# One block-diagonal product for two heads: a change in the attention stage of a fused attention and expert kernel

## The chip, the cores and the metric

The kernel runs on one core of one Trainium2 chip. Its time is the device time in microseconds of one execution. The time before is the median of three timed runs, 858.31 us. A profiled execution, recorded by the hardware profiler, gives the trace from which all rows below are taken.

The core has a matrix engine (PE; its weight loads, which overlap the products, are listed as PEld), a vector engine (DVE), a scalar engine (ACT), a general engine (POOL), a queue engine that issues most transfers (SP), and 16 DMA engines. Each engine runs its instructions in program order and waits where an operand isn't there yet.

## The reference

Three layers follow each other, all in 32-bit floats.

- Attention on q, k, v of 4 batches, 8 heads, 576 positions, 64 columns. It is the sum of two attentions. One works on means over groups of 4 positions (144 of them), and its output is repeated 4 times. The other is local: each position looks at the positions less than 4 away.
- A mixture of 8 experts on the 2,304 tokens of 512 columns: logits of the normalised token, the best expert, its softmax weight, two matrix products with a relu between them.
- A dense layer: 512 to 2,048, leaky relu, 2,048 to 512.

```python
out_d = sm_attn(q_d, k_d, v_d)             # on means of 4 positions
out_up = np.repeat(out_d, factor, axis=2)
mask = np.abs(pos[:, None] - pos[None, :]) < factor
...
out_local = np.matmul(attn, v)
return (out_up + out_local).astype(np.float32)
```

## The kernel before

The program has two stages. Up to about 189 us it does attention and the choice of experts (the routing), then the experts and the dense layer, where PE works without pause.

**Order.** The attention stage runs in an order written out by hand: the string `ORDER`, a list of items such as `LV.6`, each a call of a small function (`todo` has the table). On PE, DVE, ACT and POOL the instructions stand in exactly this order. Transfers on SP also follow the order in which they are called, and SP waits at each until its buffer is free. Items behind `at(...)` calls later in the program are sorted by planned times; they belong to the second stage.

**Local attention.** The 2,304 tokens are 18 tiles of 128. A tile has 4 strips of 32 positions; each strip looks at a window of 38 positions. Heads are handled as 4 pairs (`n`), head `n` and head `n + 4`; the member of the pair is `s`. `S.t` computes the scores, `SMX`, `SSB`, `SEX`, `SSM`, `SNM` the softmax, `LT.t` transposes it (PE) and `LTE.t` evicts it as `leT` (ACT): the 64 rows of member 0 stand on partitions 0 to 63, those of member 1 on 64 to 127. `LV.t` (`lo_pv`) adds two things in one PSUM tile `psLV`:

- the reduced attention's output for these tokens, repeated 4 times by a product with a 0/1 matrix (`rep_w`, or `rem_w` for the last 16 groups of a batch), in two parts (`dn_h` and `dn_l`, which together carry the value in the format of the fast products). These are called the carry products here;
- the local product: for each pair, member and strip a product of 64 rows by 32 array columns with v's window, 64 columns moving. Each 32-bit product is recorded as two, so these are 64 products of a tile.

`LX.t` (`lo_x`) copies the result to the tile `xt`, `LAD.t` stores it, `X`, `XE`, `L`, `LG`, and for each three tiles `LD` (picks the expert), `PF` (ranks, on PE), `PD`, `SC` route the tokens.

**v's windows.** `vw.g` (`load_vw`) loads the windows of 9 strips, half a batch, into one of three buffers `vws`, 10 or 12 transfers on SP. Group g serves strips 9g to 9g + 8: LV.2 reads groups 0 and 1, LV.4 groups 1 and 2, LV.6 groups 2 and 3, LV.15 groups 6 and 7. The buffers are cleared once by DVE at the start.

**Reduced attention.** `ds.b.u` (`dn_score`) computes scores of a batch's half, `dm`, `db`, `dx` the softmax, `dT`, `dE` transpose it, `dv.b.u` (`dn_pv`, L439 and L445) multiplies with v's means, `do`, `dh`, `dl` scale and split the output.

**Spare products.** `keep` makes products with zeros whose result nobody reads. `NW` of them (22) run before the first data arrive; an item with `+n` runs n more ahead of its own products. 8 stand before `T.0.0.0.0`, 15 before `LV.17`, 7 before `PF.17`; the 4 named at `XT.0` are never issued, since that function has no such call.

**First expert's weights.** `WL.u` loads quarter u (0 to 3) of the first expert's weights into one of two raw buffers, `WH.u.i.c` (ACT) and `WO.u.i.c` (DVE) split it into two fast parts in a buffer of 16 KB per partition (`w_unit`). Quarters 0 and 1 lie in a pool `wa` with two buffers, opened at `early`; quarters 2 and 3 in `wb`, opened at `cut`, when the attention's memory is given back. `XT`, `XH`, `XO` prepare the first tokens, `L1`, `RL`, `RO`, `L2` compute.

Of the kernel before, what the change touches and what calls it, by code (L numbers as in the profile page):

```python
# [21 lines left out]
NP = H // 2  # L22
# [31 lines left out]
O = dict(QM=(0, 0, 1, 1), NQ=8, NQD=2, NDE=0, NC=0, NVD=2, NVW=3, NES=3, NW=22, TO=12, TS=11, HB=2, XF=4, XL=3.0, WL=4,  # L54
# [3 lines left out]
qk.0.0.0 ce cv qk.0.1.0 vg.0.1 qk.0.0.1 qk.1.1.1 emb cm qk.0.1.1 cr vg.0.0 T.0.0.0.0+8 qk.1.0.1 T.0.0.0.2 E.0.0.0.0  # L58
# [14 lines left out]
E.2.1.1.1 L.3 db.1.1 S.7 SNM.6 LTE.4 LG.3 P.2.1.1 dv.1.0 dx.1.1 ds.2.0 v.2.0 SMX.7 dT.1.1.0 do.1.0 T.2.0.1.1 dE.1.1.0
SSB.7 dT.1.1.1 E.2.0.1.1 dT.1.1.2 dh.1.0 SEX.7 S.8 dm.2.0 dE.1.1.2 dl.1.0 X.1 dE.1.1.1 P.2.0.1 db.2.0 T.3.1.0.0 XE.1
dv.1.1 SMX.8 dx.2.0 E.3.1.0.0 SSB.8 v.2.1 T.3.1.1.0 SSM.7 SEX.8 dT.2.0.0 LAD.1 T.3.1.0.2 do.1.1 LAD.0 dE.2.0.0 ds.2.1
vg.3.0 E.3.1.0.2 E.3.1.1.0 qk.3.0.1 dh.1.1 SSM.8 dT.2.0.1 LAD.2 T.3.1.1.1 dE.2.0.1 dl.1.1 T.3.0.0.0 LAD.3 SNM.8 L.1
vg.3.1 E.3.1.1.1 dm.2.1 T.3.0.0.1 SNM.7 E.3.0.0.0 LV.5 LG.1 E.3.0.0.1 db.2.1 dv.2.0 LX.5 LD.2 v.3.0 dx.2.1 LV.4 LAD.5
# [5 lines left out]
SSM.10 SQ.7 LT.9 XE.7 SP.8 PF.5 dm.3.0 T.3.0.1.2 LTE.9 S.12 PD.5 SNM.10 E.3.0.1.2 L.7 db.3.0 SC.5 LT.10 LG.7 T.3.0.1.1
SMX.12 dx.3.0 LV.9 LAD.7 RN.8 early LTE.10 SSB.12 E.3.0.1.1 SEX.12 dT.3.0.0 LD.8 LX.9 LT.11 dE.3.0.0 LV.10 LAD.9
SSM.12 P.3.0.1 SQ.9 LTE.11 LM.8 S.14 LE.8 LX.10 SE.8 PF.8 SNM.12 X.9 LAD.10 SQ.10 SMX.14 ds.3.1 PD.8 XM XE.9 SSB.14
dT.3.0.1 SC.8 dm.3.1 LT.12 SEX.14 LV.11 dE.3.0.1 SSM.14 LTE.12 db.3.1 X.10 vw.6 LX.11 dv.3.0 XE.10 SNM.14 X.11 SQ.11
do.3.0 L.9 dx.3.1 SP.11 S.13 XE.11 RN.11 dT.3.1.0 LG.9 SMX.13 dh.3.0 L.11 dE.3.1.0 SSB.13 dT.3.1.1 LAD.11 dl.3.0 LG.11
# [10 lines left out]
WO.3.1.0 L2.3 WO.3.0.1 RL.5 RO.5 WO.3.0.0 L1.4 XB L1.7 RL.4 RO.4 L2.4 L1.6 L2.5 GB BT.0 RL.7 RL.6 BT.1 RO.7 BH.0 RO.6
BT.2 BH.1 BO.0 L2.6 BO.1 BH.2 BO.2 BT.3 L2.7 BH.3 BO.3
# [10 lines left out]
def tile_kernel(ctx, tc, q, k, v, emb, tau, w1, w2, win, wout, out):  # L110
# [51 lines left out]
    with man:  # L162
# [28 lines left out]
        vws = [ac.tile([P, NP, GS, D], F32, name="vw%d" % i) for i in range(O['NVW'])]  # L191
# [119 lines left out]
        def load_vw(g):  # L311
# [3 lines left out]
            for s in range(2):  # L315
                part = t[64 * s:64 * s + 64]
# [67 lines left out]
        def dn_score(b, u):  # L384
            ps = psA.tile([P, 2, 512], F32, name="psD", tag="A")
            idle(ps[:, 0, 0:256], dn_score, b, u)
            for r in range(2):
                for c in range(0, P, 64):
                    for s in range(2):
                        T.matmul(ps[c:c + 64, s, r * GR:(r + 1) * GR], qd[b][64 * s:64 * s + 64, 2 * u + r, c:c + 64],  # L390
                                 kd[b][64 * s:64 * s + 64, 2 * u + r, :], start=True, stop=True)
            if u:
                for n in range(NP):
                    for s in range(2):
                        T.matmul(ps[32 * n:32 * n + 32, s, 2 * GR:3 * GR],
                                 qd[b][64 * s:64 * s + 64, n, GR - 32:], kd[b][64 * s:64 * s + 64, n, :],
                                 start=True, stop=True)
            sps[b, u] = ps
# [31 lines left out]
        def dn_pv(b, u):  # L430
# [109 lines left out]
        def lo_pv(t):  # L540
# [9 lines left out]
            for s in range(2):  # L550
                for z, (b, r, p0) in enumerate(segs):
                    for w, src in enumerate((dn_h[b], dn_l[b])):
                        if r < 4 * P:
                            T.matmul(ps[:, s, 0:256], rep_w[:, HW + r - p0:HW + r - p0 + P],
                                     src[:, 0:DM].rearrange("p (i a d) -> p a i d", i=2, a=2)[:, s],
                                     start=z == 0 and w == 0, stop=False, skip_group_check=True)
                        else:
                            for n in range(NP):
                                T.matmul(ps[:, s, n * D:(n + 1) * D], rem_w[:, n, HW - p0:HW - p0 + P],
                                         src[:, DM + s * D:DM + (s + 1) * D],  # L560
# [753 lines left out]
```

## Time and profile before

| | |
|---|---|
| timed runs | 859.88, 858.31, 855.56 us; median 858.31 |
| profiled execution | 853.95 us |
| its span, first to last instruction | 852.2 us |
| mean granted clock of PE | 0.971 |
| PE, busy share and products | 95%, 7,887 |
| DVE, ACT, POOL, busy share | 54%, 40%, 25% |
| bytes moved | 97.88 MB |

A busy share is a mean over both stages. PE's products are pipelined, and a busy PE isn't a PE at its peak. Two products that follow each other are compared by their starts. A row of the timeline merges neighbouring instructions of one kind: start, length of the whole group, engine, line, what is written from what, rows and columns, number, and in brackets the idle time before the group with what ended it. "Issue" there means that nothing which the profile shows was awaited.

### The profile page before, as it was taken

The numbers are of one execution on the slowest core, as the hardware profiler recorded it, in microseconds if no ns is written. First come the engines' busy times: TensorE is split into PE (matmuls) and PEld (weight loads), VectorE is DVE, ScalarE is ACT, GpSimd is POOL, SyncE is SP. The second block draws the span as 40 slices with busy tenths as digits, with TensorE's granted clock in tenths as the row PEclk, the third lists the DMA queues.
The fourth block names the chain that finished last, engine by engine and source line by source line (L and its number), as shares of the span: only waits on it lengthen the run. The fifth ranks groups of instructions, "written<-read, shape, count | busy, mean of one in ns | idle before, by whom it ended". The sixth has DMA issues, their size and how long they took to land. (4 is left out here: it accounts for less than half of the span.)

```text
span 852.2 us, 19006 instructions
## 1 busy us (share of the span) xinstructions
PE 810.4 (95%) x7887; PEld 742.1 (87%) x7887; DVE 462.5 (54%) x902; ACT 337.2 (40%) x686; POOL 210.7 (25%) x244
## 2 busy tenths in 40 slices
PE   7878999789999999999999999999999999999995
PEld 6767787679999999999997789999999999999994
DVE  6646655544377988897579992332332232232222
ACT  3445645544454555656433232322223222222221
POOL 8465534234033234323023420101001001001001
PEclk9989978979999999999999999999999999999998
DMA  9779654545476787797634410111011011000001
GB/s 266 172 173 193 157 124 98 140 131 123 102 267 191 258 237 212 237 293 238 211 113 125 136 50 1 37 38 38 1 38 38 0 38 38 1 1 38 0 1 40
DMA packets 104652, 97.88 MB, mean 115 GB/s; under 512 B 58956, under 2 KB 83148, under 8 KB 104562
## 3 DMA queue, kind: packets, MB, share of 16 engines
q1 hardware_dynamic: 94018, 69.88, 29.8%
q0 software_dynamic: 10544, 26.74, 9.9%
q8 instruction: 64, 1.05, 0.5%
q14 instruction: 26, 0.21, 0.1%
HBM read 81.48 MB, written 15.12 MB: 113 GB/s over the span
## 5 line engine op out<-in xcount | busy, mean ns | idle before, releaser
L923 PE MATMUL psh<-xhi,w 128*128 128x384 f32 (+9 forms) x672 | 215.9, 321 | 0.0
L924 PE MATMUL psh<-xlo,w 128*128 128x384 f32 (+9 forms) x672 | 215.6, 321 | 0.0
L925 PE MATMUL psh<-xhi,w 128*128 128x384 f32 (+9 forms) x672 | 215.2, 320 | 0.0
L955 DVE SCALAR_TENSOR_TENSOR hs<-hs 128x384 f32<-128x384 f32 x96 | 61.9, 645 | 185.8 <-ACT hs L954 185.8
L923 PEld LDWEIGHTS psh<-xhi,w 128*128 128x128 f32 x672 | 127.7, 190 | 4.0
L924 PEld LDWEIGHTS psh<-xlo,w 128*128 128x128 f32 x672 | 127.7, 190 | 3.9
L925 PEld LDWEIGHTS psh<-xhi,w 128*128 128x128 f32 x672 | 127.6, 190 | 0.0
L954 ACT COPY hs<-psh 128x384 f32<-128x384 f32 x96 | 45.9, 478 | 194.5 <-PE psh L925 191.6
L1008 PE MATMUL pso<-w,hh 128*128 128x512 f32 x282 | 112.9, 400 | 3.7 <-ACT hh L960 3.1
L1009 PE MATMUL pso<-w,hh 128*128 128x512 f32 x282 | 110.9, 393 | 0.0
L1039 POOL DMA_INDIRECT out_dram<-o,tk x18 | 18.0, 999 | 320.9 <-ACT o L1038 315.4
L869 DVE TENSOR_TENSOR w<-r,w 128x1024 fp32r<-128x1024 f32 (+1 forms) x72 | 83.1, 1159 | 11.0 <-ACT w L866 10.6
L960 ACT CAST hh<-hs 128x384 fp32r<-128x384 f32 x94 | 48.2, 513 | 93.2 <-DVE hs L955 93.2
L996 PE MATMUL psy<-hh,w 128*128 128x192 f32 (+8 forms) x288 | 81.9, 306 | 0.0
L1006 PE MATMUL pso<-w,hl 128*128 128x512 f32 x282 | 80.8, 393 | 0.0
L997 PE MATMUL psy<-hh,w 128*128 128x192 f32 (+8 forms) x288 | 79.4, 298 | 0.0
L911 POOL TENSOR_TENSOR ds<-r 128x512 f32<-128x512 f32 x32 | 42.5, 1327 | 145.8 <-DVE r L909 63.5
L961 DVE TENSOR_TENSOR hl<-hs,hh 128x384 fp32r<-128x384 f32 x94 | 52.4, 557 | 45.8 <-ACT hh L960 45.8
L975 ACT ACTIVATE hh<-psh 128x192 fp32r<-128x192 f32 (+8 forms) x72 | 29.2, 405 | 110.4 <-PE psh L925 107.3
L866 ACT CAST w<-r 128x1024 fp32r<-128x1024 f32 (+1 forms) x72 | 67.6, 947 | 3.5 <-DMA r<-in_moe_w_dram 3.5
L1008 PEld LDWEIGHTS pso<-w,hh 128*128 128x128 f32 x282 | 52.9, 188 | 16.9 <-ACT hh L960 7.9
L1006 PEld LDWEIGHTS pso<-w,hl 128*128 128x128 f32 x282 | 53.0, 188 | 12.9 <-DVE hl L961 0.3
(230 smaller groups left out, 1255.2 us busy)
## 6 DMA issues: line engine op xcount, KB each, us to landing
r<-in_moe_w_dram SPq DMA_DIRECT2D x64, 512.0 KB
r<-in_moe_w_in_dram POOLq DMA_DIRECT2D x16, 512.0 KB, 5.3
r<-in_moe_w_out_dram POOLq DMA_DIRECT2D x16, 512.0 KB, 5.0
vw<-in_v_dram SPq DMA_DIRECT2D x64, 96.0 KB
vg<-in_v_dram SPq DMA_DIRECT2D x8, 576.0 KB
x_d<-xt SPq DMA_DIRECT2D x18, 256.0 KB
yc<-yT_d SPq DMA_DIRECT2D x6, 768.0 KB
qk<-in_q_dram SPq DMA_DIRECT2D x4, 576.0 KB
```

The source lines that it names most:

```text
L866: A.copy(w[:, 0, i, cs], src)
L869: V.tensor_tensor(out=w[:, 1, i, cs], in0=src, in1=w[:, 0, i, cs].bitcast(F32), op=ALU.subtract)
L923: T.matmul(ps, lh, rh, start=start, stop=False)
L924: T.matmul(ps, lh, rl, start=False, stop=False)
L925: T.matmul(ps, ll, rh, start=False, stop=stop)
L955: V.scalar_tensor_tensor(out=hs, in0=hs, scalar=0.01, in1=hs, op0=ALU.mult, op1=ALU.max)
L961: V.tensor_tensor(out=gl[:, 0:n], in0=hs, in1=gh[:, 0:n].bitcast(F32), op=ALU.subtract)
L996: T.matmul(ps, wh, hh[:, 0:n], start=f == 0, stop=False, skip_group_check=True)
L997: T.matmul(ps, wl, hh[:, 0:n], start=False, stop=False, skip_group_check=True)
L1006: T.matmul(ps, hl[:, c], wh, start=False, stop=f == NF2 - 1, skip_group_check=True)
L1008: T.matmul(ps, hh[:, c], wh, start=f == 0, stop=False, skip_group_check=True)
L1009: T.matmul(ps, hh[:, c], wl, start=False, stop=False, skip_group_check=True)
```

## The change

- In `lo_pv` the two heads of a pair are one product. v's window becomes a tile with the two members on a block diagonal (member s on partitions 64 s to 64 s + 63 and in columns 64 s to 64 s + 63, zeros elsewhere), the weights are all 128 rows of `leT`, and 128 columns move. The carry products take both members at once as well, so one PSUM bank holds the tile's output in the order pair, member, column. `dn_pv` writes its heads in that order, and `lo_x` puts them back.
- `dn_score` uses weights of 128 columns in place of two times 64.
- The buffers of v's windows are twice as large, and there are two of them instead of three. In the order, group 1 is loaded where group 2 was, and groups 2, 3, 5 and 7 are each loaded just behind the last product that reads the buffer: `LV.2 vw.2`, `LV.4 vw.3`, `LV.7 vw.5`, `LV.13 vw.7`. Group 4 stays behind LV.6 and group 6 goes just behind LV.11.
- To make room, `wa` has one buffer until `cut`, and quarter 1 of the first expert's weights goes to a new pool `wc` opened there. Its conversions `WH.1.*` and `WO.1.*`, which stood among the items of tiles 15 to 17, now stand together behind `XH.3` and ahead of `LD.17`.
- The counts `+8`, `+15`, `+4` and `+7` are gone. The 22 spare products ahead of the first load stay.

The order string is cut here to the items that matter; nothing else in it moves but these.

```diff
-O = dict(QM=(0, 0, 1, 1), NQ=8, NQD=2, NDE=0, NC=0, NVD=2, NVW=3, NES=3, NW=22, TO=12, TS=11, HB=2, XF=4, XL=3.0, WL=4,
+O = dict(QM=(0, 0, 1, 1), NQ=8, NQD=2, NDE=0, NC=0, NVD=2, NVW=2, NES=3, NW=22, TO=12, TS=11, HB=2, XF=4, XL=3.0, WL=4,
...
-qk.0.0.0 ce cv qk.0.1.0 vg.0.1 qk.0.0.1 qk.1.1.1 emb cm qk.0.1.1 cr vg.0.0 T.0.0.0.0+8 qk.1.0.1 T.0.0.0.2 E.0.0.0.0
+qk.0.0.0 ce cv qk.0.1.0 vg.0.1 qk.0.0.1 qk.1.1.1 emb cm qk.0.1.1 cr vg.0.0 T.0.0.0.0 qk.1.0.1 T.0.0.0.2 E.0.0.0.0
...
-WH.1.0.0 LAD.16 X.16 SQ.16 WO.1.0.0 XE.16 XR WH.1.0.1 LTE.17 WO.1.0.1 LG.14 LV.17+15 WH.1.1.1 LD.14 WH.1.1.0 WO.1.1.1
...
+XO.2 LG.17 XH.3 WH.1.0.0 WO.1.0.0 WH.1.0.1 WO.1.0.1 WH.1.1.1 WH.1.1.0 WO.1.1.1 WO.1.1.0 LD.17 XO.3 PF.17 LM.17 L1.0
...
-        vws = [ac.tile([P, NP, GS, D], F32, name="vw%d" % i) for i in range(O['NVW'])]
+        vws = [ac.tile([P, NP, GS, 2, D], F32, name="vw%d" % i) for i in range(O['NVW'])]
...
-                part = t[64 * s:64 * s + 64]
+                part = t[64 * s:64 * s + 64, :, :, s]
...
-                for c in range(0, P, 64):
-                    for s in range(2):
-                        T.matmul(ps[c:c + 64, s, r * GR:(r + 1) * GR], qd[b][64 * s:64 * s + 64, 2 * u + r, c:c + 64],
-                                 kd[b][64 * s:64 * s + 64, 2 * u + r, :], start=True, stop=True)
+                for s in range(2):
+                    T.matmul(ps[:, s, r * GR:(r + 1) * GR], qd[b][64 * s:64 * s + 64, 2 * u + r, 0:P],
+                             kd[b][64 * s:64 * s + 64, 2 * u + r, :], start=True, stop=True)
...
-                        T.matmul(o[c:c + 64, n, :], eT[:, n, kc, c:c + 64], vd[b][:, kc, head(2 * u + n % 2, n // 2), :],
+                        T.matmul(o[c:c + 64, 2 * (n % 2) + n // 2, :], eT[:, n, kc, c:c + 64], vd[b][:, kc, head(2 * u + n % 2, n // 2), :],
...
+            for z, (b, r, p0) in enumerate(segs):
+                for w, src in enumerate((dn_h[b], dn_l[b])):
+                    first = z == 0 and w == 0
+                    if r < 4 * P:
+                        T.matmul(ps[:, 0], rep_w[:, HW + r - p0:HW + r - p0 + P], src[:, 0:DM],
+                                 start=first, stop=False, skip_group_check=True)
+                    else:
+                        for n in range(NP):
+                            T.matmul(ps[:, 0, 2 * n * D:2 * (n + 1) * D], rem_w[:, n, HW - p0:HW - p0 + P],
+                                     src[:, DM:DM + 2 * D], start=first and n == 0, stop=False, skip_group_check=True)
...
-                for s in range(2):
-                    for c, b, sg, w0 in strips(t):
-                        w = vwt[b * (NSTRIP // GS) + sg // GS][:, :, sg % GS]
-                        T.matmul(ps[32 * c:32 * c + 32, s, n * D:(n + 1) * D],
-                                 eT[64 * s:64 * s + 64, n, 32 * c:32 * c + 32], w[64 * s:64 * s + 64, n, :],
-                                 start=False, stop=True, skip_group_check=True)
+                for c, b, sg, w0 in strips(t):
+                    w = vwt[b * (NSTRIP // GS) + sg // GS]
+                    T.matmul(ps[32 * c:32 * c + 32, 0, 2 * n * D:2 * (n + 1) * D], eT[:, n, 32 * c:32 * c + 32],
+                             w[:, n, sg % GS].rearrange("p s d -> p (s d)"), start=False, stop=True, skip_group_check=True)
...
-            on("LX").copy(x.rearrange("p (s c) -> p s c", s=2), st_.pop(('V', t))[:, :, 0:256])
+            on("LX").copy(x.rearrange("p (s n d) -> p n s d", s=2, d=D),
+                          st_.pop(('V', t))[:, 0].rearrange("p (n s d) -> p n s d", s=2, d=D))
...
-            for nm, bufs in (("wa", 2), ("xa", 1), ("rp", 1)):
+            for nm, bufs in (("wa", 1), ("xa", 1), ("rp", 1)):
...
-            for nm, bufs in (("wb", 2), ("wf", 4), ("rr", 2), ("xb", 1), ("hp", 2)):
+            for nm, bufs in (("wb", 2), ("wf", 4), ("rr", 2), ("xb", 1), ("hp", 2), ("wc", 1)):
...
-                nm = ("wa", "wb")[made["w"] // 2 % 2]
+                nm = ("wa", "wc", "wb", "wb")[made["w"] % 4]
```

## Rows read from the trace of the kernel before

**Rows 1.** Windows: each engine's busy us (instructions), clock, DMA share, GB/s.

```profile
6.00:188.90 182.90, 155.69 (x4022) 133.22 (x4019) 103.04 (x280) 94.09 (x217) 89.48 (x123) 0.90 0.65 158
188.90:852.00 663.10, 649.95 (x3841) 605.18 (x3840) 355.19 (x619) 241.84 (x468) 116.11 (x109) 0.99 0.33 102
```

**Rows 2.** Waits of PE before 189 us: total us, times, longest.

```profile
PE psLV L567 <- issue: 6.4, 3, 5.1
PE psS L496 <- issue: 4.0, 6, 1.6
PE psL L611 <- issue: 3.4, 1, 3.4
...
PE psDV L439 <- issue: 2.2, 1, 2.2
PE psDV L445 <- issue: 2.0, 2, 1.6
```

**Rows 3.** Timeline of PE, the second part of tile 0's local product.

```profile
49.36 0.79 PE L567 MATMUL psLV<-vw,leT 64*32 64x64 f32 x34 [5.08 <-issue]
```

**Rows 4.** Windows, between two stops of PE.

```profile
98.58:108.70 10.12, 8.53 (x255) 7.43 (x256) 6.62 (x18) 5.12 (x12) 7.71 (x8) 1.00 0.39 85
```

**Rows 5.** DMA queues of the page: packets, MB, share.

```profile
q8 instruction: 64, 1.05, 0.5%
```

**Rows 6.** Windows of five half-clock stretches: two of them and the sum.

```profile
110.40:120.50 10.10, 10.10 (x179) 9.46 (x179) 3.49 (x12) 3.81 (x11) 2.90 (x4) 0.50 0.46 124
165.00:168.30 3.30, 3.30 (x76) 3.05 (x74) 1.89 (x7) 2.48 (x6) 0.51 (x1) 0.50 0.56 146
...
sum 29.70, PE 29.70 PEld 26.34 DVE 9.09 ACT 13.67 POOL 12.04; mean PE 5.94 PEld 5.27 DVE 1.82 ACT 2.73 POOL 2.41
```

**Rows 7.** Timeline of PE at full clock.

```profile
83.17 0.66 PE L445 MATMUL psDV<-vd,deT 128*32 128x65 f32 x32
...
88.62 0.28 PE L554 MATMUL psLV<-dnl,rep_w 128*128 128x256 f32 x1
88.83 0.86 PE L567 MATMUL psLV<-vw,leT 64*32 64x64 f32 x64
89.61 1.15 PE L439 MATMUL psDV<-vd,deT 128*64 128x65 f32 x32
90.70 0.63 PE L559 MATMUL psLV<-dnh,rem_w 128*128 128x64 f32 x4
91.17 0.61 PE L559 MATMUL psLV<-dnl,rem_w 128*128 128x64 f32 x4
...
94.68 0.66 PE L155 MATMUL psX<-ident,xt 128*128 128x128 f32 x4
...
100.41 1.13 PE L567 MATMUL psLV<-vw,leT 64*32 64x64 f32 x64
```

**Rows 8.** Timeline of SP: eight of the transfers of group 7 of v's windows.

```profile
121.23 1.88 SPq L319 DMA_DIRECT2D vw<-in_v_dram  x4
...
124.92 1.86 SPq L319 DMA_DIRECT2D vw<-in_v_dram  x4
```

**Rows 9.** Timeline of PE, tiles 16 and 17.

```profile
174.02 1.19 PE L567 MATMUL psLV<-vw,leT 64*32 64x64 f32 x64
175.13 1.11 PE L155 MATMUL psX<-ident,xt 128*128 128x128 f32 x4
...
177.75 2.23 PE L180 MATMUL psLV<-dum,ones 128*128 128x256 bf16 x15
179.74 0.36 PE L554 MATMUL psLV<-dnh,rep_w 128*128 128x256 f32 x1
```

**Rows 10.** DMA issues: count, median us to landing.

```profile
out_dram<-o,tk POOLq DMA_INDIRECT x18, 2.7
```

**Rows 11.** Timeline of DVE: four conversions of half a unit.

```profile
198.58 2.48 DVE L869 TENSOR_TENSOR w<-r,w 128x512 fp32r<-128x512 f32 x4
```

**Rows 12.** Groups by line, DVE: count, busy us, mean ns, idle before.

```profile
L196 DVE MEMSET vw<- 128x2304 f32 x3 | 5.9, 1978 | 1.3 <-issue 1.3
```

More of the change, by code (lines that the diff above doesn't have):

```diff
@@ L73 @@
[L73 to L77, printed above, removed]
+E.2.1.1.2 SSB.6 LT.5 XE.2 ds.1.1 RN.2 LTE.5 SEX.6 L.2 dm.1.1 dT.1.0.1 LG.2 T.2.1.1.1 dE.1.0.1 SSM.6 LT.4 E.2.1.1.1 L.3
@@ new lines @@
+db.1.1 S.7 SNM.6 LTE.4 LG.3 P.2.1.1 dv.1.0 dx.1.1 ds.2.0 v.2.0 SMX.7 dT.1.1.0 do.1.0 T.2.0.1.1 dE.1.1.0 SSB.7 dT.1.1.1
+E.2.0.1.1 dT.1.1.2 dh.1.0 SEX.7 S.8 dm.2.0 dE.1.1.2 dl.1.0 X.1 dE.1.1.1 P.2.0.1 db.2.0 T.3.1.0.0 XE.1 dv.1.1 SMX.8
+dx.2.0 E.3.1.0.0 SSB.8 v.2.1 T.3.1.1.0 SSM.7 SEX.8 dT.2.0.0 LAD.1 T.3.1.0.2 do.1.1 LAD.0 dE.2.0.0 ds.2.1 vg.3.0
+E.3.1.0.2 E.3.1.1.0 qk.3.0.1 dh.1.1 SSM.8 dT.2.0.1 LAD.2 T.3.1.1.1 dE.2.0.1 dl.1.1 T.3.0.0.0 LAD.3 SNM.8 L.1 vg.3.1
+E.3.1.1.1 dm.2.1 T.3.0.0.1 SNM.7 E.3.0.0.0 LV.5 LG.1 E.3.0.0.1 db.2.1 dv.2.0 LX.5 LD.2 v.3.0 dx.2.1 LV.4 vw.3 LAD.5
@@ L83 @@
[L83 to L87, printed above, removed]
@@ L98 @@
[L98 to L99 removed]
+dE.2.1.1 T.3.1.0.1 SMX.11 T.3.1.1.2 E.3.1.0.1 X.6 SSB.11 SNM.9 E.3.1.1.2 dv.2.1 P.3.1.0 v.3.1 SEX.11 P.3.1.1 T.3.0.0.2
+L.5 E.3.0.0.2 LV.8 do.2.1 XE.6 LG.5 LD.5 dh.2.1 L.6 P.3.0.0 LX.8 LT.7 SSM.11 LG.6 T.3.0.1.0 SQ.8 X.8 LM.5 LTE.7 S.10
+dl.2.1 E.3.0.1.0 SNM.11 LAD.8 LV.7 vw.5 LE.5 LAD.6 SMX.10 XE.8 SE.5 SSB.10 L.8 LX.7 ds.3.0 SEX.10 X.7 LG.8 SSM.10 SQ.7
@@ new lines @@
+LT.9 XE.7 SP.8 PF.5 dm.3.0 T.3.0.1.2 LTE.9 S.12 PD.5 SNM.10 E.3.0.1.2 L.7 db.3.0 SC.5 LT.10 LG.7 T.3.0.1.1 SMX.12
+dx.3.0 LV.9 LAD.7 RN.8 early LTE.10 SSB.12 E.3.0.1.1 SEX.12 dT.3.0.0 LD.8 LX.9 LT.11 dE.3.0.0 LV.10 LAD.9 SSM.12
+P.3.0.1 SQ.9 LTE.11 LM.8 S.14 LE.8 LX.10 SE.8 PF.8 SNM.12 X.9 LAD.10 SQ.10 SMX.14 ds.3.1 PD.8 XM XE.9 SSB.14 dT.3.0.1
+SC.8 dm.3.1 LT.12 SEX.14 LV.11 vw.6 dE.3.0.1 SSM.14 LTE.12 db.3.1 X.10 LX.11 dv.3.0 XE.10 SNM.14 X.11 SQ.11 do.3.0 L.9
+dx.3.1 SP.11 S.13 XE.11 RN.11 dT.3.1.0 LG.9 SMX.13 dh.3.0 L.11 dE.3.1.0 SSB.13 dT.3.1.1 LAD.11 dl.3.0 LG.11 dT.3.1.2
@@ new lines @@
+SEX.13 L.10 dE.3.1.1 SSM.13 S.15 dE.3.1.2 SNM.13 LG.10 dv.3.1 LD.11 SMX.15 LT.13 LM.11 SSB.15 LE.11 PF.11 LV.12 do.3.1
+SEX.15 LTE.13 PD.11 dh.3.1 S.16 LX.12 dl.3.1 CF LAD.12 SQ.12 LT.14 SSM.15 LV.13 vw.7 LTE.14 FE SNM.15 X.12 SE.11 LX.13
+WL.0 LT.15 SMX.16 XE.12 SC.11 X.13 WL.1 SSB.16 LTE.15 CS L.12 FC LAD.13 SEX.16 LV.14 SQ.13 SSM.16 LG.12 XE.13 S.17
+LX.14 L.13 SNM.16 LAD.14 SQ.14 SMX.17 X.14 LG.13 SP.14 SSB.17 LT.16 XE.14 LV.15 RN.14 SEX.17 WH.0.0.0 SSM.17 LTE.16
+L.14 WO.0.0.0 SNM.17 WH.0.1.0 LV.16 LX.15 WO.0.1.0 IA WH.0.0.1 X.15 LAD.15 SQ.15 WO.0.0.1 LT.17 LX.16 LAD.16 X.16
@@ new lines @@
+SQ.16 XE.16 XR LTE.17 LG.14 LV.17 LD.14 XE.15 PF.14 LM.14 LX.17 L.15 PD.14 L.16 LE.14 LAD.17 cut SQ.17 X.17 SE.14
+LG.15 SP.17 LG.16 XG SC.14 WH.0.1.1 RN.17 XT.0 XE.17 XT.1 WO.0.1.1 XH.0 XT.2 WL.2 XH.1 L.17 XO.0 XH.2 XO.1 XT.3 WL.3
+XO.2 LG.17 XH.3 WH.1.0.0 WO.1.0.0 WH.1.0.1 WO.1.0.1 WH.1.1.1 WH.1.1.0 WO.1.1.1 WO.1.1.0 LD.17 XO.3 PF.17 LM.17 L1.0
+PD.17 LE.17 SE.17 L1.1 RL.0 SC.17 RO.0 L2.0 RL.1 RO.1 WH.2.0.0 CA L1.2 WO.2.0.0 WH.2.0.1 WH.2.1.0 RK L2.1 WH.2.1.1
+RL.2 L1.3 RO.2 WO.2.0.1 WH.3.0.0 WO.2.1.1 WH.3.1.1 L2.2 WO.2.1.0 WH.3.1.0 RL.3 WO.3.1.1 L1.5 WH.3.0.1 IB RO.3 WO.3.1.0
@@ L100 @@
+L2.3 WO.3.0.1 RL.5 RO.5 WO.3.0.0 L1.4 XB L1.7 RL.4 RO.4 L2.4 L1.6 L2.5 GB BT.0 RL.7 RL.6 BT.1 RO.7 BH.0 RO.6 BT.2 BH.1
+BO.0 L2.6 BO.1 BH.2 BO.2 BT.3 L2.7 BH.3 BO.3
 """
@@ L549, in lo_pv @@
                 segs.append((b, r, p0))
-            for s in range(2):
[L551 to L560, printed above, removed]
-                                         start=z == 0 and w == 0 and n == 0, stop=False, skip_group_check=True)
```

20 lines of the change are left out of this document (3 added, 17 removed).

## Prediction

> **What bounds the kernel now.** I read first the windows of the two stages [rows 1]. From 188.9 us to the end PE is busy 650 of 663 us at a clock of 0.99, and the change touches nothing that runs there. The attention stage before it, 182.9 us, is where a gain or a loss must arise. PE is busy 155.7 us of it, no other engine more than 103, and the mean granted clock is 0.90. So the stage is PE's program order: its work, plus the times in which PE stands still, plus what the lower clock adds.
>
> Second, the waits of PE up to 189 us [rows 2]. Five rows are waits for "issue", in which nothing that the profile shows is missing: 6.4 + 4.0 + 3.4 + 2.2 + 2.0 = 18.0 us in 13 waits. The reader is to see that these lie inside runs of products of one kind: the local product of tile 0 stops 5.08 us with half its products done [rows 3]. Between two such stops PE started 255 products and 256 weight loads [rows 4], the third number in that row being DVE's. The two stages hold 7,863 products and 7,859 weight loads [rows 1], and the instruction queue brought 64 packets and 1.05 MB [rows 5]: one packet for 15,722 / 64 = 246 instructions of PE. I read the stops as late instructions: when PE runs through a packet's worth faster than the next arrives, it stands still.
>
> Third, the clock [rows 6]. Five stretches of 29.7 us together ran at 0.50, which is 1.2 of 2.4 GHz; each begins during or just behind one of those stops. The same local product takes 0.78 us from its first start to the next group's at full clock (88.83 to 89.61) and 1.11 us at half (174.02 to 175.13) [rows 7, 9], so half clock costs between 30% of a stretch and, for work bound by columns, 50%. I use 40%.
>
> **The change part by part.** *Local product.* 64 recorded products of 64 columns become 32 of 128 per tile, on all 128 rows and 32 array columns. Half of each moving row is zero. The shape isn't in the trace. Nearest: 32 products of L445, same rows and width but 65 columns, take 0.66 us; 32 of L439, 64 wide, hence two side by side where 32 wide leaves room for four, with half our columns, take 1.15 us [rows 7]. If columns bind, 65 / 2 = 32.5 and 128 / 4 = 32 are the same work, so 1.15 is the price; if they don't, 0.66. Now it is 0.86. I take columns: +0.29 in a full-clock tile, and twice 1.15 against 1.19, +1.1, in a half-clock one. With 16 tiles at full clock and 2 at half that is 4.6 + 2.2 = **+6.8 us** (bounds: 18 x (0.66 - 0.86) = -3.6, and +8.5 with four at half).
>
> The Trainium skill (TensorEngine Tiling (Array Packing), Tiling Modes, Available Configurations) lists eight independent tiles for 64 x 32 and four for 128 x 32, and under Performance Considerations asks for row tiling when the contraction is 64. By it alone the group would go from 0.86 to 1.72 us, +15.5 in all, and the sum below would end at +2.9 instead of -5.8; the rows above put it at 1.15, and it is a rival below.
>
> *Carry products.* The products with the remainder weights (16 per tile in four tiles, 64 columns) become 8 of 128. Four of 64 columns follow each other in 91.17 - 90.70 = 0.47 us, 0.118 each, and one of 256 columns is followed after 0.21 us by another kind [rows 7]. At 0.118 the saving is 4 x 8 x 0.118 = **-3.8 us**; at 0.21, none. I take the first, since a 256-column one costs so little more. The other 72 become 36 of twice the columns: zero.
>
> *Scores of the reduced attention.* 8 products per call become 4 of 128 columns of weights, moving columns unchanged, two tiles abreast where there were four: zero. By L439's rate (32 products two abreast, 1,040 columns in a row, in 1.15 us) the 8 recorded products of 144 columns take 0.64 us two abreast, and if they no longer overlapped 0.64 more in each of eight calls, +5.
>
> *Spare products.* 8 at the start and 7 ahead of the first expert fill waits for the first data and for LD.17: zero, or 15 x 0.13 = -2.0 if they don't, by the rate of the others. Those 15, of tile 17, stand between 177.75 and 179.74 [rows 9], ahead of that tile's carry products, which need only data that is long there: **-2.0 us**.
>
> *Instructions.* 18 x 32 + 64 + 36 + 32 + 30 = 738 products go, and as many weight loads: 1,476, or 6 of the stage's 33 packets (8,041 instructions [rows 1]). 182.9 - 18.0 = 165 us of unstopped time over 33 packets is 5.0 us each, over 27 it is 6.1. So each stop shortens by about 1.1 us. The longest, 5.1, 3.4, 2.2, 1.6 and 1.6 [rows 2], would leave 4.0 + 2.3 + 1.1 + 0.5 + 0.5 = 8.4; the other eight, 4.1 together, go. **-9.6 us** (bounds 0 and -18). Of the five half-clock stretches those of 10.1 us (behind one of the 1.6 us stops) and of 3.3 us (behind stops under 1 us) [rows 6] should go: 13.4 x 0.4, **-5.4 us** (bounds 0 and 29.7 x 0.4 = -12; the new wait below may bring one of 3.3 us back, +1.3).
>
> *Two buffers for vw.* Group 3 of v's windows may now load only when LV.4 has read group 1. LV.6 reads it. SP issues the 10 transfers that LV.6 needs in 126.78 - 121.23 = 5.55 us for group 7, the nearest such load [rows 8]; landing isn't shown for them, and of the transfers with one shown the shortest is 2.7 us [rows 10]. That makes 8.2 us from LV.4's end. PE's own work from there (94.68) to LV.6 (100.41) is 5.7 - 1.6, the stop in L496, = 4.1 us [rows 2, 7]. PE waits about **+4.1 us** at LV.6, at most 6 if SP is slower, nothing if PE is late by then; everything behind in PE's order waits with it. On SP the stores of tiles 5 and 4 and group 4 stand behind, needed much later. Group 7, now behind LV.13, is needed by LV.15 and stands ahead of the first expert's weights on SP: the way between is longer, **+0.5** (0 to 3). Groups 2 and 5 have slack; 4 and 6 waited for the same tile before.
>
> *Second weight unit.* Its four conversions now stand on DVE between tile 17's logits and LD.17, which picks the expert and whose result PE wants before the first expert product. Four on DVE run 2.48 us, 0.62 each [rows 11], and the first starts behind one of ACT's, taken as long: **+3.1 us** on the end of the stage. ACT and DVE lose them earlier, where PE sets the pace: zero. WL.3 then issues later on SP, but its weights are converted only after two expert blocks: zero.
>
> *Clearing vw.* Two of 4,608 columns for three of 2,304: one more 1.98 us [rows 12] on DVE, ahead of the first evictions. The first loads cover most: **+0.5** (0 to 2). The eviction lo_x and the reordered dn columns move the same elements: zero.
>
> Sum: 6.8 - 3.8 - 2.0 - 9.6 - 5.4 + 4.1 + 0.5 + 3.1 + 0.5 = **-5.8 us**. The profiled execution took 853.95 (852.2 of span and 1.75 around it), so 848.1. It was quicker than all three timed runs (855.56 to 859.88); on their median, 858.31, the sum gives **852.5**.
>
> **Rivals.** *Fewer instructions bring no relief* (slower). If the stops come from transfers that crowd the queues, the next packet is as late as before, and stops and clock stay: -5.8 + 9.6 + 5.4 = +9.2, 867.5. For it: the DMA engines are busy 0.65 of this stage against 0.33 after it [rows 1]. Against: between stops lie packets' worths of instructions. It decides from a relief, stops and clock together, below 4.9 us (9.2 - 4.9 = 4.3, half a per cent). The Trainium skill (Runtime: NRT & Kernel Launch, Instruction fetch mechanics) has the sequencer fetch the next block of instructions during the current one and calls the boundary's cost mostly hidden; by that rule fewer instructions give nothing. The trace disagrees where it stops 5.08 us at one.
>
> *Other waits fill the freed time* (no change). PE runs ahead and meets operands that DVE, ACT and POOL finish in their own order; a third of the 15.0 of relief lost is +5.0: 857.5. For it: DVE is busy 103 and ACT 94 of 182.9 us [rows 1]. Against: few of PE's waits are for them now. Losing the full clock behind the removed 15 would do the same: 5 us at half, +2.
>
> *The local product doubles* (no change). If its columns bind it already, it takes 2 x 0.86: +15.5 for +6.8, 861.2. Against: eight abreast its 64 x 64 / 8 = 512 columns in a row are half of L439's 1,040, and would take 0.57 of its 0.86 us.
>
> *Columns don't bind the local product* (faster). -3.6 for +6.8: -16.2, 842.1. For it: L445's rate; against: L439's.
>
> **How the numbers follow.** Forecast 0.46 (848 to 857 by itself), no relief 0.17, other waits 0.20, doubled product 0.04, cheap product 0.13. Within 0.5% is 4.3 us, 854.0 to 862.6, about what this kernel's timing can tell from no change. Faster: 0.13 and two thirds of the forecast, 0.31, whose centre lies 1.5 us beyond the bound: 0.44. Same: the other 0.15 and 0.24 of the two rivals without change, 0.39. Slower: 0.17. The range 842 to 866 reaches to the cheap product at one end and nearly to "no relief" at the other, and leaves out half of each, 0.15.
>
> **What would show it.** Right: PE's "issue" waits below 10 us, fewer half-clock stretches, the local group near 1.15 us with 32 products, a wait of LV.6 for vw of some 4 us, four conversions in a row ahead of LD.17. Wrong: issue waits near 18 us, a local group near 0.66, or long waits of PE for ACT, DVE or vw elsewhere.

## The result and the profile after

The changed kernel took 844.93 us (median of 6 runs, 841.77 to 847.84), the kernel before 859.10 beside it (852.76 to 861.86): a ratio of 0.9853 with a 95% interval of 0.9811 to 0.9894. Two later measurements gave 0.9853 (0.9818 to 0.9888) and 0.9887 (0.9848 to 0.9925). The gain is about 1.4%, some 12.6 us by the ratio and 14.2 between the medians. In a further stretch of runs, on another chip, the changed kernel itself didn't run, and three close variants of it gained 0.0 to 0.6%; so the size of the gain isn't shown for every chip. The forecast was 852.5 us, a gain of 5.8: right in its direction and inside its range, but the gain came out more than twice as large as the sum.

The profiled execution of the changed kernel took 845.36 us. Windows of its two stages:

```profile
6.00:181.10 175.10, 147.57 (x3283) 119.45 (x3277) 105.16 (x281) 94.81 (x217) 89.85 (x123) 0.90 0.69 162
181.10:843.00 661.90, 648.57 (x3841) 603.56 (x3839) 355.13 (x619) 242.19 (x468) 116.25 (x108) 0.99 0.33 103
```

Against [rows 1] the attention stage has lost 7.8 us of its 182.9, and the expert stage is where it was. PE is busy 8.1 us less in the first, with 739 products fewer.

Waits of PE in the attention stage of the changed kernel, to be held against [rows 2], and the instruction queue's line of its page, against [rows 5]:

```profile
PE psLV L563 <- DMA vw<-in_v_dram: 6.2, 4, 4.6
PE psR L651 <- DVE oh L627: 4.4, 1, 4.4
PE psx L155 <- ACT xe L802: 3.6, 2, 3.1
PE psX L155 <- issue: 2.6, 1, 2.6
PE psLV L563 <- issue: 2.0, 2, 1.6
...
PE psS L495 <- issue: 1.7, 1, 1.7
...
PE psDT L155 <- issue: 0.5, 1, 0.5
PE psLT L155 <- issue: 0.4, 1, 0.4
PE psDV L438 <- issue: 0.2, 1, 0.2
```

```profile
q8 instruction: 58, 0.95, 0.5%
```

The stops called issue add up to 2.6 + 2.0 + 1.7 + 0.5 + 0.4 + 0.2 = 7.4 us in 7 waits; they were 18.0 in 13. Six instruction packets are gone. In their place stand three waits for operands: for the windows of v, for the routing of the last tile (`oh`), and for the gathered tokens of the first expert (`xe`).

Timeline of PE around LV.4 and LV.6 of the changed kernel, which answers to [rows 7]:

```profile
83.26 0.66 PE L557 MATMUL psLV<-dnh,rem_w 128*128 128x128 f32 x4
83.76 0.61 PE L557 MATMUL psLV<-dnl,rem_w 128*128 128x128 f32 x4
84.21 0.45 PE L553 MATMUL psLV<-dnh,rep_w 128*128 128x512 f32 x1
84.49 0.40 PE L553 MATMUL psLV<-dnl,rep_w 128*128 128x512 f32 x1
84.82 1.08 PE L563 MATMUL psLV<-vw,leT 128*32 128x128 f32 x32
85.83 0.66 PE L155 MATMUL psX<-ident,xt 128*128 128x128 f32 x4
...
89.83 0.42 PE L563 MATMUL psLV<-vw,leT 128*32 128x128 f32 x6
94.85 0.66 PE L563 MATMUL psLV<-vw,leT 128*32 128x128 f32 x8 [4.60 <-DMA vw<-in_v_dram]
95.73 0.66 PE L563 MATMUL psLV<-vw,leT 128*32 128x128 f32 x8 [0.23 <-DMA vw<-in_v_dram]
96.87 0.65 PE L563 MATMUL psLV<-vw,leT 128*32 128x128 f32 x8 [0.49 <-DMA vw<-in_v_dram]
98.45 0.64 PE L563 MATMUL psLV<-vw,leT 128*32 128x128 f32 x2 [0.92 <-DMA vw<-in_v_dram]
99.01 1.03 PE L607 MATMUL psL<-enT,xT 128*64 128x8 f32 x16
```

Three things are to be seen. From its first start to the next group's the local product takes 85.83 - 84.82 = 1.01 us, where 64 products took 0.78. The remainder products start 0.48 us apart for four of 128 columns, as four of 64 did (0.47). And LV.6 begins at 89.83, runs 6 products, and needs 9.2 us because its window isn't there.

The half clock behind that, in windows (the clock is the third column from the end):

```profile
93.20:103.30 10.10, 6.81 (x118) 4.58 (x119) 0.20 (x1) 2.54 (x6) 5.04 (x5) 0.50 0.72 161
...
171.70:185.30 13.60, 7.29 (x48) 6.52 (x49) 7.34 (x27) 6.19 (x15) 4.87 (x5) 0.50 0.65 156
```

The first stretch at 1.2 GHz begins within the 4.60 us wait, the second within the wait for the gathered tokens, and the routing wait lies inside it. So half clock follows waits for operands here just as it followed the stops. PE isn't busy through all of these stretches, though: 6.81 of 10.10 us and 7.29 of 13.60, where in [rows 6] it was busy 29.70 of 29.70. The mean clock of the stage stayed at 0.90.

### The profile page after: what moved, and what is told of

Its sections match the earlier page's. It is cut to its first block, busy times and chain, and to the rows that moved or that the text cites. A ratio compares the mean times of both kernels' runs of the same rounds, so it can differ in the third digit from the quotient of the medians.

```text
span 843.5 us, 17561 instructions
## 1 busy us (share of the span) xinstructions
PE 800.9 (95%) x7149; PEld 726.6 (86%) x7149; DVE 464.5 (55%) x901; ACT 338.3 (40%) x686; POOL 211.2 (25%) x244
## 5 line engine op out<-in xcount | busy, mean ns | idle before, releaser
L971 ACT ACTIVATE hh<-psh 128x192 fp32r<-128x192 f32 (+8 forms) x72 | 29.2, 406 | 107.0 <-PE psh L921 103.6
```

## The experiments

All kernels compute the whole result. The runs lie in three stretches on three chips, in which the kernel before took 850.7, 857.8 and 861.3 us; kernels are compared within one stretch. The first had no run of the changed kernel, so its four kernels can be held against each other and against the kernel before alone. Three of them are the changed kernel but for small moves, and their ratios there are 0.9938 to 0.9996; for the two of these that ran again in the third stretch they are 0.9853 and 0.9867. What made the kernel before quicker in the first stretch stays open.

**The changed kernel again**, in the second and third stretch.

> The changed kernel itself again, beside the kernel before on the same chip, so that the other kernels of this study have a ratio to be held against. Theory A (the gain is in the program and not in the place where it ran): a ratio of 0.981 to 0.990, that is 835 to 842 us where the kernel before takes 850.7. Rival G (part of the first gain was chance, since the stops for instructions differ from run to run): a ratio of 0.990 to 0.997.

845.22 us, ratio 0.9853: A. The profile shows the first expert product at 175.3 us, earlier than in the first profile, and almost no wait for a window. Timeline of PE at LV.6 of this run:

```profile
89.58 0.28 PE L495 MATMUL psS<-qkT 64*32 64x38 f32 x9 [2.00 <-issue]
...
91.36 0.99 PE L563 MATMUL psLV<-vw,leT 128*32 128x128 f32 x22
92.81 0.97 PE L563 MATMUL psLV<-vw,leT 128*32 128x128 f32 x10 [0.45 <-DMA vw<-in_v_dram]
```

A stop of 2.00 us just ahead lets LV.6 start at 91.36 instead of 89.83, and SP has issued the window's last transfer at 92.07 instead of 93.53; the window is nearly there.

> The changed kernel once more, as the neighbour of the next three. The kernel before has taken 850.7 us in one stretch of this study and 857.8 in another. Theory A (the ratio belongs to the programs): 0.981 to 0.990 to the kernel before here too. Rival G (where DMA or fetches run otherwise, the gain is smaller): over 0.990, with PE waiting 6 us or more for windows of v as in the first profile.

849.45 us, ratio 0.9887 (0.9848 to 0.9925). The median lies in A's band, the interval holds both. No wait for windows here either, so G's sign is absent.

**The two heads apart again**, in the first and the third stretch. The windows, the order and the conversions stay as in the changed kernel; `lo_pv`, the copy and `dn_pv` are those of the kernel before:

```diff
-                for c, b, sg, w0 in strips(t):
-                    w = vwt[b * (NSTRIP // GS) + sg // GS]
-                    T.matmul(ps[32 * c:32 * c + 32, 0, 2 * n * D:2 * (n + 1) * D], eT[:, n, 32 * c:32 * c + 32], ...
+                for s in range(2):
+                    for c, b, sg, w0 in strips(t):
+                        w = vwt[b * (NSTRIP // GS) + sg // GS][:, :, sg % GS, s]
+                        T.matmul(ps[32 * c:32 * c + 32, s, n * D:(n + 1) * D],
+                                 eT[64 * s:64 * s + 64, n, 32 * c:32 * c + 32], w[64 * s:64 * s + 64, n, :], ...
```

> This kernel keeps the windows of v in their diagonal layout, the order without the spare products and the two conversions, but takes the products of lo_pv, the copy of lo_x and the output order of dn_pv from the kernel before: 64 local products of 64 columns for a tile instead of 32 of 128, the carry products one for each head, 1,360 PE instructions more than the changed kernel. Theory A (the gain is stops for instructions): the work of PE moves by about -4 us for the local product (18 tiles at 0.79 for 1.01 a group) and +3.8 for the carry products, which cancel, and the stops that the profile calls issue go back from 7.4 to about 17 us before the first expert product, so the kernel gives back most of the gain and takes 852 to 858 us. Rival B (the number of instructions is free, and the gain came from the shorter carry products and the missing spare products): the stops stay under 10 us and the kernel takes 842 to 849 us.

855.73 us, ratio 1.007 (1.0036 to 1.0104) where the spare-product kernel beside it had 0.9996. The records hold 644 products more than the changed kernel's and as many weight loads, 1,288 instructions (the expectation counted 1,360). Waits of PE before its first expert product:

```profile
PE psLV L566 <- issue: 11.8, 4, 6.0
...
PE psS L495 <- issue: 4.1, 2, 3.3
```

The stops are back: 16.6 us in all (shorter rows are the rest), the longest 6.0 us, once more within tile 0's local product:

```profile
50.28 0.44 PE L566 MATMUL psLV<-vw,leT 64*32 64x64 f32 x10 [6.00 <-issue]
```

The place of this stop tells its cause. Here it comes when 54 of the 64 products are done, in the kernel before when 30 are [rows 3], and in the kernel before without its spare products, a run told below, when 38 are:

```profile
43.32 0.64 PE L567 MATMUL psLV<-vw,leT 64*32 64x64 f32 x38
50.52 0.66 PE L567 MATMUL psLV<-vw,leT 64*32 64x64 f32 x26 [6.55 <-issue]
```

That kernel issues 8 spare products fewer ahead of this place, and the one with the heads apart 16 score products fewer besides. So the stop keeps its count, behind the 854th recorded product in all three, and not its place in the program. Between seven pairs of stops of the kernel before lie 382, 255, 380, 128, 255, 127 and 126 products: multiples of 128, but for a few records, and with the weight loads multiples of 256 instructions. The packets of the instruction queue have records too. In the 5.08 us stop of the kernel before there is one (queues between 44.3 and 49.36 us):

```profile
q8 instruction: 1, 0.02, 1.5%
```

It lands at 47.76, and PE goes on 1.60 us later. Eleven of that kernel's 13 stops, 16.8 of their 18.0 us, end 1.2 to 1.7 us behind the landing of such a packet, and 7 of the 8 here, 16.4 of 16.6 us. These stops are waits for instructions. In the three profiles of the changed kernel 3.5, 5.9 and 5.2 us of the stops end so. The cause of the other 3.7, 4.0 and 6.5 us isn't shown; the longest of them, 2.0 to 2.6 us, stands behind the 2,955th product in all three.

> The kernel with the two heads apart in the products again (1,288 PE products' worth of instructions more, as before), now beside the changed kernel. Theory A (stops for instructions): 8 to 13 us slower than the changed kernel, with stops called issue of 14 us or more in all before the first expert product, though its local groups take 0.2 us less each. Rival B (instructions are free): within 3 us of the changed kernel.

859.34 us against 849.45 of the changed kernel beside it, +9.9, and a ratio to the kernel before of 0.999 (0.9956 to 1.0024). The profile, of its longest execution (867.72 us), shows 21.4 us of issue stops. Theory A, against B. With the products taken apart the whole gain is gone, although the diagonal windows, two buffers, joined score products, moved conversions and missing spare products are all still in. The joined products carry the gain. The rest adds up to nothing that can be measured here, and in the first stretch to a loss of 0.7% (1.007). How the 9.9 us divide between the local and the carry products is known from the next run alone; the local product wasn't taken apart by itself.

**Only the carry products apart.**

```diff
-                        T.matmul(ps[:, 0], rep_w[:, HW + r - p0:HW + r - p0 + P], src[:, 0:DM],
-                                 start=first, stop=False, skip_group_check=True)
+                        for u in range(2):
+                            T.matmul(ps[:, 0, 256 * u:256 * u + 256], rep_w[:, HW + r - p0:HW + r - p0 + P],
+                                     src[:, 256 * u:256 * u + 256], start=first and u == 0, ...
...
+                            for s in range(2):
+                                T.matmul(ps[:, 0, (2 * n + s) * D:(2 * n + s + 1) * D], rem_w[:, n, HW - p0:HW - p0 + P], ...
```

> The changed kernel with only the carry products taken apart again by head: two products of 256 columns for one of 512, and two of 64 for one of 128, 208 PE instructions more, same columns and same results. Theory A (the join of the carry products saved 3.8 us): 2 to 5 us slower than the changed kernel. Rival H (columns set their time, so that the join saved under 1 us): within 1.5 us of it.

With 68 products more by the records (136 instructions, not 208), 850.75 us, 5.5 more than the changed kernel beside it (ratios 0.9896, 0.9859 to 0.9933, and 0.9853; the intervals overlap, and over the 6 runs of each the means differ by 5.0 with an uncertainty of about 3.5, worked out from their spread). The tile of batch 2's end in its timeline, and the same place of the changed kernel's first profile:

```profile
146.56 1.06 PE L559 MATMUL psLV<-dnh,rem_w 128*128 128x64 f32 x8
147.45 1.06 PE L559 MATMUL psLV<-dnl,rem_w 128*128 128x64 f32 x8
148.34 0.36 PE L554 MATMUL psLV<-dnh,rep_w 128*128 128x256 f32 x1
```

```profile
143.73 0.64 PE L557 MATMUL psLV<-dnh,rem_w 128*128 128x128 f32 x4
144.21 0.61 PE L557 MATMUL psLV<-dnl,rem_w 128*128 128x128 f32 x4
144.66 0.45 PE L553 MATMUL psLV<-dnh,rep_w 128*128 128x512 f32 x1
```

Sixteen products in 1.78 us against eight in 0.93: 0.85 us a tile, 3.4 in four tiles. A product of 64 columns takes 0.111 us here, one of 128 takes 0.116. The time lies at the upper edge of A's 2 to 5 us, and H's 1.5 just at the end of the uncertainty; what decides against H is the price in the rows. The stops add up to 7.3 us in this profile, no more than in the changed kernel's, so the loss isn't in them.

**The spare products**, out of the kernel before alone, and back in the changed kernel (`T.0.0.0.0+8`, `LV.17+15`, `PF.17+7`).

> The kernel before with its spare products at the first transpose group (8), LV.17 (15), the gather (4) and the first prefix product (7) taken out, and nothing else changed. Theory A: only the 15 of LV.17 stand on the path, so 1 to 3 us less than the kernel before. Rival D (they carry most of the gain): 6 us less or more. Rival C (they cover waits): no change or slower.

857.90 us, ratio 0.9993 (0.9960 to 1.0026): none of the gain is theirs. Its profile, of an execution of 858.97 us, shows 22.9 us of issue stops. Of these 6.9 us are 19 short ones below 0.5 us, where the kernel before has 1.7 us in 5; the longer ones add up to 16.0 us here and to 16.3 there, 8 in each.

> The changed kernel with the spare products of the kernel before put back at the first transpose group (8), at LV.17 (15) and at the first prefix product (7). Theory A: 30 products more, of which only the 15 of LV.17 stand on the path, so +2 us: 845 to 849 us. Rival C (the spare products hid waits or kept the clock, so that taking them out cost time): 1 us or more faster than the changed kernel, with less time at half clock. Rival D (the spare products made most of the gain): 850 us or more.

850.28 us in the first stretch, ratio 0.9996 (0.9967 to 1.0025), which can't be judged without the changed kernel beside it. Hence again:

> The changed kernel with 30 spare products back, now beside the changed kernel. Theory A: at most 2 us slower, as taking them from the kernel before changed nothing that could be measured (ratio 0.9993). Rival D (they cost more in the changed kernel, where they stand ahead of other waits): 4 us slower or more.

847.77 us against 849.45, ratios 0.9853 (0.9813 to 0.9893) and 0.9887: no loss. D falls. A's 2 us can't be told from none, neither here nor in the kernel before.

**The wait for vw.3**: tiles 4 and 5 exchanged and the load right behind LV.4. One line of the order is shown; the later items of the two tiles are exchanged likewise.

```diff
-E.3.1.1.1 dm.2.1 T.3.0.0.1 SNM.7 E.3.0.0.0 LV.5 LG.1 E.3.0.0.1 db.2.1 dv.2.0 LX.5 LD.2 v.3.0 dx.2.1 LV.4 vw.3 LAD.5
+E.3.1.1.1 dm.2.1 T.3.0.0.1 SNM.7 E.3.0.0.0 LV.4 vw.3 LG.1 E.3.0.0.1 db.2.1 dv.2.0 LX.4 LD.2 v.3.0 dx.2.1 LV.5 LAD.4
```

> The changed kernel with tiles 4 and 5 in the other order through their local attention (4 first), and the clearing and loading of the window vw.3 right behind LV.4, so that its buffer comes free one tile earlier. In the changed kernel PE waits 6.2 us in LV.6 for this load, and about 10 us at half clock follow. Theory A (that wait is on the path of the stage): the wait goes, the first expert product comes 4 to 7 us earlier and the kernel takes 838 to 842 us. Rival E (the time goes to the next wait, at the routing or at the conversions of expert weights): the wait of LV.6 goes, the first expert product moves by under 2 us, and the time is 843 to 847 us.

845.79 us in the first stretch, ratio 0.9954 (0.9925 to 0.9983). Its profile, of the quickest execution (838.87 us), has no wait at LV.6, and one of 3.3 us for a later window; the first expert product comes at 175.3 us. The time is in E's band and the 5.8 us at the first expert product in A's, so this run decides nothing. Beside the changed kernel:

> The changed kernel with tiles 4 and 5 exchanged and vw.3 one tile earlier, now beside the changed kernel. Theory A (where PE waits for vw.3, the wait is on the path): as much less time as the changed kernel's profile here shows of that wait and of the half clock behind it, 4 us or more if it shows 5 us. Rival E (the time goes to the next load of a window, or to the gather and the routing behind the last tile): within 2 us.

848.62 us against 849.45, within E's 2 us. The changed kernel's profile there showed no wait for vw.3, so A had nothing to give and E isn't told from it; but the exchanged order didn't even prevent the wait. Timeline of SP and of PE in this run, and then SP's in the changed kernel's first profile:

```profile
77.93 5.07 SPq L572 DMA_DIRECT2D x_d<-xt  x2
83.09 0.36 SPq L304 DMA_DIRECT2D vg<-in_v_dram  x1
83.56 3.04 SPq L319 DMA_DIRECT2D vw<-in_v_dram  x4
...
88.09 4.66 SPq L319 DMA_DIRECT2D vw<-in_v_dram  x4
```

```profile
89.58 0.42 PE L563 MATMUL psLV<-vw,leT 128*32 128x128 f32 x6
95.61 1.68 PE L563 MATMUL psLV<-vw,leT 128*32 128x128 f32 x24 [5.61 <-DMA vw<-in_v_dram]
```

```profile
82.92 0.36 SPq L304 DMA_DIRECT2D vg<-in_v_dram  x1
85.26 2.44 SPq L319 DMA_DIRECT2D vw<-in_v_dram  x4
87.79 0.80 SPq L323 DMA_DIRECT2D vw<-in_v_dram  x2
88.64 3.99 SPq L319 DMA_DIRECT2D vw<-in_v_dram  x4
```

The load could start one tile earlier, but SP reaches it 1.7 us earlier only, behind two stores and a load of means, and then issues its transfers more slowly. The window is there no sooner (95.61 against 94.85). My step that LV.4's end sets this load was half the matter: SP's queue is the other half.

**The conversions behind SE.17**: `WH.1` and `WO.1` moved from ahead of `LD.17` to behind `SE.17`.

```diff
-XO.2 LG.17 XH.3 WH.1.0.0 WO.1.0.0 WH.1.0.1 WO.1.0.1 WH.1.1.1 WH.1.1.0 WO.1.1.1 WO.1.1.0 LD.17 XO.3 PF.17 LM.17 L1.0
+XO.2 LG.17 XH.3 LD.17 XO.3 PF.17 LM.17 L1.0 PD.17 LE.17 SE.17 WH.1.0.0 WO.1.0.0 WH.1.0.1 WO.1.0.1 WH.1.1.1 WH.1.1.0 ...
```

> The changed kernel with the eight conversions WH.1 and WO.1 moved from ahead of LD.17 to behind SE.17. In the changed kernel DVE works through four conversions of 2.5 us while PE waits 4.4 us for the routing of the last tile. Theory A: that wait goes and the first expert product comes 3 to 4.4 us earlier; the second expert's weights have 10 us of first-expert products as cover, so the time is 840 to 843 us. Rival F (the conversions are late then for the second expert, and their wait moves there): the first expert product comes earlier, but PE waits as much ahead of the second expert's products, and the time is 844 to 850 us.

846.09 us, ratio 0.9938 (0.9905 to 0.9970), again without its neighbour; 4 us below the spare-product kernel of its stretch, as the exchanged order is. The time is in F's band, and the profile, of an execution of 851.00 us, shows F's sign: PE waits 0.8 us for the routing, but 3.3 us for `hh` (L971) behind the first expert product, where the changed kernel had no such wait. Both moves together, beside the changed kernel:

> The changed kernel with both orders moved: tiles 4 and 5 exchanged with vw.3 right behind LV.4, and the conversions WH.1 and WO.1 behind SE.17. Theory A (both waits are on the path and add): 5 to 8 us less than the changed kernel in the same stretch of runs. Rival E (the time goes to the next load of a window and to the second expert): within 2 us of the changed kernel.

845.34 us against 845.22, ratios 0.9850 (0.9809 to 0.9891) and 0.9853: E. With an uncertainty of about 4 us, A's 5 to 8 us are excluded and a gain of 2 isn't. The routing wait of this kernel, and the wait for `hh` behind its first expert product:

```profile
PE psR L651 <- DVE oh L627: 0.8, 1, 0.8
PE psy L992 <- ACT hh L971: 0.5, 1, 0.5
```

The routing wait fell from 4.4 to 0.8 us, yet the first expert product stands at 175.9 us, no earlier than the 175.3 of the changed kernel beside it. The first gathered tokens are transposed at 171.0 against 167.1, so the stage ahead had lost as much as the routing gave; one profile of each doesn't tell that from chance. No version shown to be better than the changed kernel came of it.

## Why the prediction was right, and where it was off

The direction is right by its mechanism, and the range in part by luck. The measured 844.93 us lies outside the 848 to 857 that the forecast gave by itself. The range holds it because its lower end, 842, came from the rival in which columns don't bind the local product, and the rows refute that rival.

One table gathers the attention stages: PE's busy time, the waits by kind and the time at half clock, worked out from the mean clock as twice (1 - clock) times the length.

| profile | first expert product, us | PE busy | issue | vw | other waits | half clock |
|---|---|---|---|---|---|---|
| before | 188.9 | 155.7 | 18.0 | 0 | 9.3 | 37 |
| before without spares | 193.3 | 154.8 | 22.9 | 0 | 9.3 | 41 |
| heads apart | 190.7 | 152.1 | 16.6 | 0 | 15.7 | 52 |
| changed, first | 181.1 | 147.6 | 7.4 | 6.2 | 13.8 | 35 |
| changed, second stretch | 175.3 | 142.8 | 9.9 | 0.5 | 15.7 | 10 |
| changed, third stretch | 180.3 | 146.7 | 11.8 | 0 | 15.0 | 21 |

**Instructions.** Right in mechanism and nearly in size: -9.6 forecast, 18.0 to a mean of 9.7 measured, -8.3. In the table every kernel with 64 recorded products a tile has 16.6 us of stops or more; those with 32, all variants above included, have 5.6 to 11.8. The forecast's 246 instructions a packet are 256 by the spacing of the stops. The Trainium skill (Runtime: NRT & Kernel Launch, Instruction fetch mechanics) has the block boundary mostly hidden; the 6.00 us stop above disagrees. The count decides where a stop can come. Whether its length follows the number of instructions or their rate in the runs of short products isn't told apart, since both fell together.

**Clock.** -5.4 forecast. In the first profile the half clock hardly fell (37 to 35 us), since new waits of 4.6 and 3.1 us start stretches as the old stops did. But half clock costs only where PE works in it. The sums of the windows of all half-clock stretches ahead of the first expert product, in the kernel before and in the first profile after:

```profile
sum 37.50, PE 36.37 PEld 31.65 DVE 12.40 ACT 15.81 POOL 15.90; mean PE 6.06 PEld 5.28 DVE 2.07 ACT 2.63 POOL 2.65
```

```profile
sum 33.40, PE 23.52 PEld 17.83 DVE 13.97 ACT 15.55 POOL 15.38; mean PE 4.70 PEld 3.57 DVE 2.79 ACT 3.11 POOL 3.08
```

PE's work at half clock fell from 36.4 us to 23.5, and to 6.0 and 16.7 in the other two profiles, 15.4 on the mean: (36.4 - 23.5) x 0.4 = -5.2 in the first profile and (36.4 - 15.4) x 0.4 = -8.4 on the mean. The step was right, and too small. The five stretches of [rows 6] leave out a sixth, from 134.2 to 141.1 us, which begins in a wait of 1.82 us for `escore` of DVE; so in the kernel before, too, half clock followed a wait for an operand.

**Local product.** Columns set most of its price: the 32 products of L445 with 65 columns [rows 7] take 0.59 us to the next group's start, the 32 with 128 take 1.01. That next group:

```profile
83.76 0.55 PE L155 MATMUL psT<-ident,qk 128*128 128x128 f32 x3
```

But it was mis-sized: 1.01 us against 0.78, not 1.15 against 0.86. The forecast took lengths of groups, where starts are what count. That is +0.23 in 16 tiles and, in a half-clock tile, about 1.7 against 1.1: 3.7 + 1.2 = +4.9 for +6.8. The Trainium skill (TensorEngine Tiling (Array Packing), Performance Considerations) asks for row tiling at a contraction of 64; the trace agrees that giving it up costs, 29% and not the double.

**Carry products, scores, clearing.** -3.8 forecast; 3.4 by the rows, 5.0 plus or minus 3.5 by the means of the run. The first score products start at 15.3 us as at 15.2 before, so the longer clearing is hidden; the 64 that replace 128 take no longer (PE busy 6.3 us with them, 6.9 before).

**Spare products.** -2.0 forecast, nothing measured in the times. By the rows PE's busy time loses some 3 us with them (15 took 2.0 us [rows 9], 7 took 0.9). With them back in the changed kernel, in the third stretch, the waits for gathered tokens and routing are 0.7 and 3.2 us, without them 3.7 and 4.4, so that these waits seem to take it up.

**New waits.** At LV.6 the forecast was +4.1 (6 at most, nothing if PE is late). The three profiles show 6.2, 0.5 and 0: each of those cases happens. The conversions were put at +3.1 and PE waits 4.4 in all three, against 0.3 before; with the conversions moved away it was 0.8. Here the rows of DVE are as forecast, four in a row ahead of the routing, which starts with L620:

```profile
177.46 2.50 DVE L865 TENSOR_TENSOR w<-r,w 128x512 fp32r<-128x512 f32 x4 [1.37 <-ACT w L862]
179.88 0.17 DVE L620 TENSOR_REDUCE rmx<-lg 128x3 f32<-128x24 f32 x1
```

The wait for gathered tokens, 3.6 to 3.8 us where [rows 2] shows nothing of its size, wasn't foreseen: PE runs ahead and meets POOL's gather. It is the rival of other waits in part.

**The sum of what was measured.** On the mean of the three profiles: stops -8.3, clock -8.4, local product +4.9, carry products -3.4, spare products -2.9, windows of v +2.2, other waits +5.5 (9.3 to 14.8). That is -10.4, and the first expert product comes 10.0 us earlier (188.9 to a mean of 178.9). The forecast had -5.8. The term that was furthest off is the clock, by 3.0; the local product was put 1.9 too high, the waits for windows (4.1 and 0.5) 2.4 too high, the other waits (3.1 and 0.5) 1.9 too low.

**The base.** Between the first two profiles the gain is 853.95 - 845.36 = 8.6 us. The prediction put the sum of one execution on the median: "on their median, 858.31, the sum gives **852.5**". That execution was 5.2 us quicker than the median of the kernel's six, the one after lies on its own; these 5.2 us are most of what lies between 8.6 and the 14.2 of the medians. A quick execution may hold less of what the change removes, so that the sum came out too small. This isn't shown: there is one profile of the kernel before, and the one without spare products, of an execution of 858.97 us, has as much in stops of half a microsecond and more (16.0 us against 16.3), and more in short ones only.

**Open.** Why the kernel before took 850.7 us in the first stretch and 858 to 861 elsewhere, while variants of the changed one stayed near 845 to 850, and so what the change would have gained there; and whether the exchanged order or the late conversions gain there, since the changed kernel didn't run in that stretch.

## What to carry to other kernels

Where a matrix engine runs through many short products and stops with nothing awaited, fewer and larger products can win although each group gets slower: here 0.23 us a tile was paid for 8 us of stops. When such a stage speeds up, count the operands that were just in time, for they are the next waits, and half clock can follow a wait for data as it follows a stop. Price half clock by the work that stands in it, not by its length. And a sum made on one profiled execution should ask how much of the removed cost that execution held; a second profile of the kernel before might have told.

## What the runs showed of the hardware beyond that

- Stops of PE came at fixed counts of its instructions, multiples of 128 products with their weight loads apart, and ended 1.2 to 1.7 us behind the landing of a packet of the instruction queue (11 of 13 in the kernel before, 7 of 8 with the heads apart).
- A 32-bit product with 128 rows and 128 columns of weights took 0.111 us with 64 columns moving and 0.116 with 128, so halving it saved nothing.
- A transfer queue that may start earlier doesn't land earlier by as much: for the same kind of load SP took from 1.85 to 5.83 us to issue four transfers, in six profiles of the changed kernel and its variants.
- The same program's stops differ from run to run: 7.4, 9.9 and 11.8 us in three profiles of one kernel, with medians of 844.9, 845.2 and 849.5 us.
